# One fused attention and two-mixture kernel on one core: how its first hundred microseconds are fed

## The chip, the cores and the metric

The kernel runs on one core of a Trainium2 chip. The engines of a core run side by side, each through its own queue in order: TensorE (PE, with PEld for its weight loads), VectorE (DVE), ScalarE (ACT), GpSimd (POOL), and SyncE (SP), which here issues the transfers. The metric is the device time of one execution in microseconds, the median of the runs shown.

## The reference

```python
def _attn_ref(q, k, v, s):          # 4 batches, 8 heads, 576 positions, 64 wide, fp32
    scores = scale * np.matmul(q, k.transpose(0, 1, 3, 2))
    cum = np.cumsum(np.maximum(s, 0.0), axis=-1)
    bias = -(cum[:, :, :, None] - cum[:, :, None, :])
    scores = np.where(causal, -1000000000.0, scores + np.minimum(bias, 0.0))
    attn = softmax(scores)
    return np.matmul(attn, v)
def _moe_ref(x, w_in, w_out):       # 2304 tokens, 512 wide, inner width 2048
    h = x @ w_in
    return (h * (1.0 / (1.0 + np.exp(-1.702 * h)))) @ w_out
def _moe2_ref(x, w_in, w_out, s, b):
    r = np.maximum(x @ w_in, 0.0)
    return (s * (r * r) + b) @ w_out
reference = moe2(moe(attention))
```

The weight matrices come in as 64-bit floats and are turned into 32-bit ones on the chip.

## The kernel before, in words

The queries of each batch are cut into a first half (320 positions) and a second (256), which gives eight units; a unit has eight heads, numbered on from unit to unit, so heads 0 to 7 are the first unit. `setup` makes the running sum of the gates, splits it into a rounded part `high` and a rest `low`, and writes these and two constant rows (`root`, `minus`) to a scratch in DRAM, `rows_d`. Each head's operands stand in a tile `raw` (64 rows of queries and keys, `qkT`) with four of these rows beside them, so that one product gives scores and bias together; `prep` loads them (L213, and `beside`, L209 and L210). The first unit's heads are multiplied in plain fp32 (from `raw`); later units use two parts, `hi` and `lo`, in the faster fp32r form.

A head passes through three stages: `qk` (score product L252, row minimum and mask on VectorE L258, exponential on ScalarE L264, scaling by the reciprocal sum), `transposes` (L290, copied out of PSUM at L294 or L296) and `pv` (L311 or L317, copied into `xraw` at L325 or L327). In a step, head n is in `qk`, head n-1 in `transposes`, head n-2 in `pv`. The first unit runs its steps alone. From then on each `run(ui)` works off the mixture of unit `ui` on TensorE and puts the attention stages of the next unit between its matmuls by a table of shares.

The mixture of a unit splits its input `xraw` into two fp32r parts, `xT` (L368 on ScalarE, L369 on VectorE), makes sixteen first-layer sums `ph` (h_item, twelve matmuls each at L385: four blocks of x by three products), and takes tanh (L390), `th` (L391) and a split `g` (L393, L394) of each. After ten of them come four second-layer sums `py` over the first eight g (y_item, L407), then six more `ph`, then the other four `py`. PSUM holds three of these sums at a time.

A weight block is converted by `load_w`: a 512 KB transfer `pair` (L129), L131 on ScalarE, L132 and L133 on VectorE, then a split into two parts, L138 on ScalarE and L139 on VectorE. The sixteen blocks of the first matrix (`wi`) come two to a step from step 1 on. Those of the second (`wo`) are all written after the first unit, ahead of `run(0)`; a staging pool of three `pair` tiles limits them.

Who sets the order: TensorE's queue is as written. SP's is as written in the first unit's steps. Everything else, the `wo` transfers included, is put in place by the framework's scheduler, and a transfer also waits for an earlier one whose completion counter it takes over (eight counters in turn).

Of the kernel before, what the change touches and what calls it, by code (L numbers as in the profile page):

```python
# [9 lines left out]
F32 = mybir.dt.float32  # L10
# [56 lines left out]
def fused_kernel(ctx: ExitStack, tc: tile.TileContext, qkT, vP, s, w1i, w1o, w2i, w2o, s2, b2, out):  # L67
# [75 lines left out]
    with ExitStack() as p1:  # L143
# [15 lines left out]
        def setup():  # L159
            cum = gp.tile([P, 2 * NMAX], F32, tag="g", name="cum")[:BH, :S]  # L160
            nc.sync.dma_start(cum, s)
            zero = gp.tile([P, 2 * NMAX], F32, tag="g", name="zero")[:BH, :S]
# [8 lines left out]
            root = gp.tile([P, 2 * NMAX], F32, tag="g", name="root")[:BH, :S]  # L171
            nc.gpsimd.memset(root, ROOT)
            minus = gp.tile([P, 2 * NMAX], F32, tag="g", name="minus")[:BH, :S]
            nc.gpsimd.memset(minus, -ROOT)
            for side, rows in enumerate(((f32(high), f32(low), minus, minus), (root, root, f32(high), f32(low)))):
                for k, row in enumerate(rows):
                    nc.sync.dma_start(rows_d[side, :, k, :], row)
            nc.sync.dma_start(s_sb, s2.partition_broadcast(P))
            nc.sync.dma_start(b_sb, b2.partition_broadcast(P))
# [18 lines left out]
        def prep(n):  # L198
# [13 lines left out]
            if n < H:  # L212
                nc.sync.dma_start(raw[:D, : u.n + J], src[:D])  # L213
                beside(raw)
            else:
                nc.sync.dma_start(raw[:, : u.n + J], src)
# [145 lines left out]
        def split_x(ui):  # L362
            u = units[ui]
            parts = []
            for cc in range(NC):
                raw = xraw.pop((ui, cc))
                x = xp.tile([P, 2, NMAX], F32R, tag="xT", name="xT")
                nc.scalar.activation(x[:, 0, : u.n], raw[:, : u.n], AF.Copy)  # L368
                nc.vector.tensor_tensor(x[:, 1, : u.n], raw[:, : u.n], f32(x[:, 0, : u.n]), ALU.subtract)  # L369
                parts.append(x)  # L370
            return parts
# [4 lines left out]

        def h_item(ui, f, x):
            n = units[ui].n
            ph = psM.tile([P, 512], F32, tag="m", name="ph1")
            w = wi[f]  # L380
            k = 0
            for cc in range(NC):
                wc = slice(cc * P, (cc + 1) * P)
                for a, b in ((1, 0), (0, 1), (0, 0)):
                    nc.tensor.matmul(ph[:, :n], w[:, a, wc], x[cc][:, b, :n], start=(k == 0), stop=(k == 3 * NC - 1))  # L385
                    k += 1
# [239 lines left out]
```

## Time and profile before

| | us |
|---|---|
| median of 3 runs | 1078.57 (1078.39, 1078.57, 1409.4) |
| profiled execution, its own time | 1075.86 |
| span in the profile, first to last instruction | 1074.1 |

The profiled execution is 2.71 us below the median. The page gives each engine's busy time over the whole span; The views by stretch show where TensorE's share is lower than over the whole; the timeline shows single instructions there.

### The profile page before, as it was taken

To read this page: it belongs to the slowest core of one execution; us is meant where nothing else is said; L and a number is where in the kernel's file an instruction comes from. 1 tells how busy PE (TensorE), PEld (TensorE's weight loads), DVE (VectorE), ACT (ScalarE), POOL (GpSimd) and SP (SyncE) were. 2 spreads that over 40 slices of the span, in tenths; PEclk is the share of its full clock that TensorE was granted. 3 is DMA by queue.
4 is the path that set the end of the run, shared out by engine and by line. 5 is a ranking of instruction groups with operands and counts; after the bars stand their busy time and mean duration, and the time that the engine had idled before them with its cause. 6 is when DMAs were issued, how large, how long until landed. Compare 5 with 4: busy or idle time off the path is not lost.

```text
span 1074.1 us, 17311 instructions
## 1 busy us (share of the span) xinstructions
PE 1020.6 (95%) x6216; PEld 912.4 (85%) x6216; DVE 641.1 (60%) x1440; ACT 536.2 (50%) x1252; POOL 347.2 (32%) x382
## 2 busy tenths in 40 slices
PE   4978999999999999999999998899999999999998
PEld 2457999999989989999999998678888888888887
DVE  4689777566468788878887488942332323232343
ACT  4797766556536646656656476632322322222222
POOL 1224445335335435445444341431301210111011
PEclk9988999999999999999999998999999999999999
DMA  6566322121032232232221187510200100000010
GB/s 200 168 236 200 102 78 77 49 82 55 8 119 73 69 104 70 82 89 71 87 85 50 41 277 236 174 50 1 79 0 1 64 1 1 35 10 1 1 40 20
DMA packets 38917, 85.51 MB, mean 80 GB/s; under 512 B 5520, under 2 KB 16144, under 8 KB 38832
## 3 DMA queue, kind: packets, MB, share of 16 engines
q1 hardware_dynamic: 38832, 84.41, 25.0%
q8 instruction: 49, 0.80, 0.3%
q14 instruction: 36, 0.29, 0.1%
HBM read 70.30 MB, written 10.03 MB: 75 GB/s over the span
## 4 chain that ended last, share of the span: by engine, by line
PE 72%; DVE 12%; ACT 5%; DMA 5%; issue 4%; POOL 1%; SPq 1%; DVEq 0%; ACTq 0%; POOLq 0%
PE py L554 17%; PE ph L506 17%; PE py L407 13%; PE ph L385 12%; PE ps L252 5%; PE pst L290 4%; PE po L317 3%; DVE hi L114 3%; DVE pair L133 1%; DMA pair<-w1i 1%; DVE x L258 1%; ACT x L264 1%; DVE pair L132 1%; DMA pair<-w2i 1%; DMA xraw<-x_d 1%
## 5 line engine op out<-in xcount | busy, mean ns | idle before, releaser
L385 PE MATMUL ph<-xT,wi 128*128 128x320 f32 (+1 forms) x1536 | 245.4, 304 | 7.1 <-ACT xT L368 3.6
L385 PEld LDWEIGHTS ph<-xT,wi 128*128 128x128 f32 x1536 | 216.5, 193 | 8.6 <-ACT xT L368 3.8
L407 PE MATMUL py<-g,wo 128*128 128x320 f32 (+1 forms) x1344 | 215.2, 304 | 1.4 <-DVE th L391 0.9
L554 PE MATMUL py<-wo,g 128*128 128x512 f32 x864 | 209.8, 392 | 5.8 <-POOL g L514 5.8
L506 PE MATMUL ph<-xT,wi 128*128 128x512 f32 (+1 forms) x960 | 208.4, 368 | 0.0
L554 PEld LDWEIGHTS py<-wo,g 128*128 128x128 f32 x864 | 162.2, 189 | 40.4 <-POOL g L514 6.8
L506 PEld LDWEIGHTS ph<-xT,wi 128*128 128x128 f32 x960 | 169.1, 188 | 31.0
L407 PEld LDWEIGHTS py<-g,wo 128*128 128x128 f32 x1344 | 187.9, 189 | 2.6 <-DVE th L391 1.0
L510 DVE TENSOR_TENSOR r<-r 128x512 f32<-128x512 f32 (+1 forms) x80 | 54.2, 678 | 209.4 <-ACT r L509 209.4
L514 POOL TENSOR_TENSOR g<-r,g 128x512 fp32r<-128x512 f32 (+1 forms) x40 | 50.1, 1252 | 314.9 <-PE py L554 170.0
L394 POOL TENSOR_TENSOR g<-th,g 128x320 fp32r<-128x320 f32 (+1 forms) x128 | 112.7, 881 | 113.2 <-ACT g L393 112.7
L264 ACT ACTIVATE x<-x,m 64x64 f32<-64x64 f32 (+2 forms) x160 | 89.5, 560 | 107.7 <-DVE m L258 105.7
L509 ACT ACTIVATE r<-ph 128x512 f32<-128x512 f32 (+1 forms) x80 | 44.3, 553 | 151.3 <-PE ph L506 151.1
L232 POOL TENSOR_TENSOR lo<-raw,hi 64x576 fp32r<-64x576 f32 (+1 forms) x56 | 67.8, 1212 | 136.6 <-issue 59.8
L258 DVE CUSTOM_DVE_ANT_0 x<-ps,mask 64x64 f32<-64x64 f32 (+2 forms) x160 | 68.1, 426 | 60.2 <-PE ps L252 58.3
L290 PE MATMUL pst<-ident,x 128*128 128x128 f32 (+2 forms) x480 | 86.3, 288 | 9.1 <-DVE ph L299 8.4
L513 ACT ACTIVATE g<-r 128x512 fp32r<-128x512 f32 (+1 forms) x80 | 47.0, 587 | 91.9 <-DVE r L511 91.9
L296 ACT ACTIVATE ph<-pst 64x256 fp32r<-64x256 f32 (+2 forms) x144 | 67.0, 472 | 23.3 <-PE pst L290 21.8
L112 POOL TENSOR_SCALAR x<-x,tot 64x64 f32<-64x64 f32 (+1 forms) x96 | 47.9, 506 | 94.1 <-DVE tot L269 70.8
L290 PEld LDWEIGHTS pst<-ident,x 128*128 128x128 f32 (+2 forms) x480 | 54.9, 136 | 24.2 <-DVE ph L299 13.4
L114 DVE TENSOR_SCALAR hi<-raw 128x832 fp32r<-128x832 f32 (+1 forms) x48 | 70.1, 1460 | 2.0 <-DMA vraw<-vP 1.8
L391 DVE SCALAR_TENSOR_TENSOR th<-th,ph 128x320 f32<-128x320 f32 (+1 forms) x128 | 57.4, 448 | 23.0 <-ACT th L390 21.9
(69 smaller groups left out, 1318.0 us busy)
## 6 DMA issues: line engine op xcount, KB each, us to landing
raw<-qkT SPq DMA_DIRECT2D x32, 416.0 KB
pair<-w1o SPq DMA_DIRECT2D x16, 512.0 KB
pair<-w1i SPq DMA_DIRECT2D x16, 512.0 KB
pair<-w2i SPq DMA_DIRECT2D x16, 512.0 KB
pair<-w2o SPq DMA_DIRECT2D x16, 512.0 KB
raw<-qkT SPq DMA_DIRECT2D x24, 320.0 KB
vraw<-vP SPq DMA_DIRECT2D x16, 320.0 KB
out<-y SPq DMA_DIRECT2D x18, 256.0 KB
```

Source lines behind the costliest of these rows:

```text
L114: nc.vector.tensor_scalar(out=out, in0=in_, scalar1=scale, scalar2=None, op0=ALU.mult)
L232: nc.gpsimd.tensor_tensor(lo[:D, kc], raw[:D, kc], f32(hi[:D, kc]), ALU.subtract)
L258: nc.vector.tensor_tensor_reduce(out=x[:w, j0:j1], in0=ps[:w, : j1 - j0], in1=mask[:w, WIDE - a0 + j0 : WIDE - a0 + j1], scale=-1.0 / ROOT ...
L264: nc.scalar.activation(x[:w, :a1], x[:w, :a1], AF.Exp, bias=least, scale=-1.0, accum_out=tot[:w, c : c + 1])
L290: nc.tensor.transpose(ps[: j1 - j0, at : at + a1 - a0], t["x"][c][: a1 - a0, j0:j1], ident[: a1 - a0, : a1 - a0])
L296: nc.scalar.activation(t["ph"][:rows, base:end], ps[:rows, :m], AF.Copy)
L385: nc.tensor.matmul(ph[:, :n], w[:, a, wc], x[cc][:, b, :n], start=(k == 0), stop=(k == 3 * NC - 1))
L391: nc.vector.scalar_tensor_tensor(out=th[:, :n], in0=th[:, :n], scalar=1.0, in1=ph[:, :n], op0=ALU.add, op1=ALU.mult)
L394: nc.gpsimd.tensor_tensor(g[:, 1, :n], th[:, :n], f32(g[:, 0, :n]), ALU.subtract)
L407: nc.tensor.matmul(py[:, :n], wo[f][:, a, wc], g_t[ui, f][:, b, :n], start=(k == 0), stop=(k == 3 * G - 1))
L506: nc.tensor.matmul(ph[:, :n], wi2[f][:, a, wc], x[cc][:, b, :n], start=(k == 0), stop=(k == 3 * NC - 1))
L554: nc.tensor.matmul(py[t], g2[k][a][:, t * P : (t + 1) * P], wo2[k][:, b, :], start=(k == 0 and i == 0), stop=(k == NF - 1 and i == 2),)
```

## The change

1. Head 0's operands no longer pass through DRAM: the constant rows and the first head's `high` and `low` rows are written from SBUF into `raw` by six small transfers, two of them issued by ScalarE. Heads 1 to 7 still read `rows_d`. Head 0's loads, one `wo` block and the constants are queued ahead; the two small loads `s_sb`, `b_sb` move behind step 1.
2. Twenty-seven matmuls (three first-layer sums over the first three blocks of x) are issued between the transposes and the `pv` of head 7. The splits of these three blocks are written there too.
3. `wo` blocks are written one per first-layer sum, in place of all sixteen ahead of `run(0)`.

```diff
--- before.py
+++ after.py
@@ -159,6 +159,18 @@
         def setup():
             cum = gp.tile([P, 2 * NMAX], F32, tag="g", name="cum")[:BH, :S]
             nc.sync.dma_start(cum, s)
+            root = gp.tile([P, 2 * NMAX], F32, tag="g", name="root")[:BH, :S]
+            nc.gpsimd.memset(root, ROOT)
+            minus = gp.tile([P, 2 * NMAX], F32, tag="g", name="minus")[:BH, :S]
+            nc.gpsimd.memset(minus, -ROOT)
+            prep_to(0)
+            u, t = units[0], heads[0]
+            raw = t["parts"][0][0]
+            nc.sync.dma_start(raw[D + 2 : R, t["kc"]], minus[:2, : u.i1])
+            nc.sync.dma_start(raw[D : D + 2, t["qc"]], root[:2, u.i0 : u.i1])
+            for k in range(2):
+                nc.sync.dma_start(rows_d[0, :, 2 + k, :], minus)
+                nc.sync.dma_start(rows_d[1, :, k, :], root)
             zero = gp.tile([P, 2 * NMAX], F32, tag="g", name="zero")[:BH, :S]
             nc.vector.memset(zero, 0.0)
             pos = gp.tile([P, 2 * NMAX], F32, tag="g", name="pos")[:BH, :S]
@@ -168,15 +180,13 @@
             nc.vector.tensor_copy(high, cum)
             low = gp.tile([P, 2 * NMAX], F32R, tag="g", name="low")[:BH, :S]
             nc.vector.tensor_tensor(low, cum, f32(high), ALU.subtract)
-            root = gp.tile([P, 2 * NMAX], F32, tag="g", name="root")[:BH, :S]
-            nc.gpsimd.memset(root, ROOT)
-            minus = gp.tile([P, 2 * NMAX], F32, tag="g", name="minus")[:BH, :S]
-            nc.gpsimd.memset(minus, -ROOT)
-            for side, rows in enumerate(((f32(high), f32(low), minus, minus), (root, root, f32(high), f32(low)))):
-                for k, row in enumerate(rows):
-                    nc.sync.dma_start(rows_d[side, :, k, :], row)
-            nc.sync.dma_start(s_sb, s2.partition_broadcast(P))
-            nc.sync.dma_start(b_sb, b2.partition_broadcast(P))
+
+            for queue, k, part in ((nc.sync, 0, high), (nc.scalar, 1, low)):
+                queue.dma_start(raw[D + k : D + k + 1, t["kc"]], f32(part)[:1, : u.i1])
+                queue.dma_start(raw[D + 2 + k : D + 3 + k, t["qc"]], f32(part)[:1, u.i0 : u.i1])
+            for k, part in enumerate((high, low)):
+                nc.sync.dma_start(rows_d[0, :, k, :], f32(part))
+                nc.sync.dma_start(rows_d[1, :, 2 + k, :], f32(part))
 
         ap, limit = None, 0
         size = {}
@@ -211,7 +221,8 @@
 
             if n < H:
                 nc.sync.dma_start(raw[:D, : u.n + J], src[:D])
-                beside(raw)
+                if n > 0:
+                    beside(raw)
             else:
                 nc.sync.dma_start(raw[:, : u.n + J], src)
             if h % 2 == 0:
@@ -359,33 +370,43 @@
             else:
                 pv(n)
 
-        def split_x(ui):
-            u = units[ui]
-            parts = []
-            for cc in range(NC):
-                raw = xraw.pop((ui, cc))
-                x = xp.tile([P, 2, NMAX], F32R, tag="xT", name="xT")
-                nc.scalar.activation(x[:, 0, : u.n], raw[:, : u.n], AF.Copy)
-                nc.vector.tensor_tensor(x[:, 1, : u.n], raw[:, : u.n], f32(x[:, 0, : u.n]), ALU.subtract)
-                parts.append(x)
-            return parts
+        def split_x(ui, cc):
+            n, raw = units[ui].n, xraw.pop((ui, cc))
+            x = xp.tile([P, 2, NMAX], F32R, tag="xT", name="xT")
+            nc.scalar.activation(x[:, 0, :n], raw[:, :n], AF.Copy)
+            nc.vector.tensor_tensor(x[:, 1, :n], raw[:, :n], f32(x[:, 0, :n]), ALU.subtract)
+            return x
 
         wi, wo = {}, {}
         g_t = {}
         y_t = {}
 
+        begun = {}
+
+        def h_sum(ph, n, f, x, blocks):
+
+            for k in range(3 * blocks.start, 3 * blocks.stop):
+                cc, (a, b) = k // 3, ((1, 0), (0, 1), (0, 0))[k % 3]
+                nc.tensor.matmul(
+                    ph[:, :n], wi[f][:, a, cc * P : (cc + 1) * P], x[cc][:, b, :n],
+                    start=(k == 0), stop=(k == 3 * NC - 1),
+                )
+                if k % 4 == 3 and k < 3 * NC - 1:
+                    yield 4 * (n / 2.4 + 3)
+
+        def h_begin(ui, f, x):
+            ph = begun[ui, f] = psM.tile([P, 512], F32, tag="m", name="ph1")
+            for _ in h_sum(ph, units[ui].n, f, x, range(len(x))):
+                pass
+
         def h_item(ui, f, x):
             n = units[ui].n
-            ph = psM.tile([P, 512], F32, tag="m", name="ph1")
-            w = wi[f]
-            k = 0
-            for cc in range(NC):
-                wc = slice(cc * P, (cc + 1) * P)
-                for a, b in ((1, 0), (0, 1), (0, 0)):
-                    nc.tensor.matmul(ph[:, :n], w[:, a, wc], x[cc][:, b, :n], start=(k == 0), stop=(k == 3 * NC - 1))
-                    k += 1
-                    if k % 4 == 0 and k < 3 * NC:
-                        yield 4 * (n / 2.4 + 3)
+            if (ui, f) in begun:
+                ph = begun.pop((ui, f))
+                yield from h_sum(ph, n, f, x, range(NC - 1, NC))
+            else:
+                ph = psM.tile([P, 512], F32, tag="m", name="ph1")
+                yield from h_sum(ph, n, f, x, range(NC))
             th = gp.tile([P, NMAX], F32, tag="th", name="th", bufs=2)
             nc.scalar.activation(th[:, :n], ph[:, :n], AF.Tanh, scale=0.851)
             nc.vector.scalar_tensor_tensor(out=th[:, :n], in0=th[:, :n], scalar=1.0, in1=ph[:, :n], op0=ALU.add, op1=ALU.mult)
@@ -418,21 +439,25 @@
                 nc.sync.dma_start(x1_d[c * P : (c + 1) * P, t0_of[ui] : t0_of[ui] + n], y[:, :n])
             yield 4 * (n / 2.4 + 3)
 
-        def mixture(ui):
-            x = split_x(ui)
+        def mixture(ui, x):
+            x += [split_x(ui, cc) for cc in range(len(x), NC)]
             for f in range(G + AHEAD):
+                if ui == 0:
+                    load_wo(f)
                 yield from h_item(ui, f, x)
             yield EARLY
             for c in range(NC):
                 yield from y_item(ui, 0, c)
             yield EARLY
             for f in range(G + AHEAD, NF):
+                if ui == 0:
+                    load_wo(f)
                 yield from h_item(ui, f, x)
             yield EARLY
             for c in range(NC):
                 yield from y_item(ui, 1, c)
 
-        def run(ui):
+        def run(ui, x):
 
             lower = H * (ui + 1) if ui in (0, B - 1) else 0
             items = []
...
@@ -454,29 +479,36 @@
 
         with tc.tile_pool(name="half0", bufs=1) as pool, tc.manual_schedule(engines={PE}):
             attention_pool(pool, B * H, 0)
+            x0 = []
             with tc.manual_schedule(engines={PE, SP}):
                 setup()
-                prep_to(0)
                 for step in range(H + 2):
                     for item in attention_items(step):
+                        if item[2] == H - 1 and item[1] == "pv":
+                            x0 += [split_x(0, cc) for cc in range(NC - 1)]
+                            for f in range(3):
+                                h_begin(0, f, x0)
                         if item[2] < H:
                             attend(item)
                     for f in range(len(wi), min(NF, 2 * step)):
                         wi[f] = load_w((wp, "wo", NF), w1i, "wi", f)
-
-            with tc.manual_schedule(engines={PE}):
-                for f in range(NF):
-                    wo[f] = load_w((pool, "pair", 3), w1o, "wo", f)
-                run(0)
+                    if step == 1:
+                        nc.sync.dma_start(s_sb, s2.partition_broadcast(P))
+                        nc.sync.dma_start(b_sb, b2.partition_broadcast(P))
+
+            def load_wo(f):
+                wo[f] = load_w((pool, "pair", 3), w1o, "wo", f)
+
+            run(0, x0)
             for ui in range(1, B - 1):
-                run(ui)
+                run(ui, [])
```

On SP at the program's start (rows of before with before's line numbers, of after with after's) the first stretch reads, before:

```order
L161 DMA cum<-s 32x576
L129 DMA pair<-w1o 128x1024 x3
L177 DMA rows_d<-high 32x576
L177 DMA rows_d<-low 32x576
L177 DMA rows_d<-minus 32x576 x2
L177 DMA rows_d<-root 32x576 x2
L177 DMA rows_d<-high 32x576
L177 DMA rows_d<-low 32x576
L178 DMA s_sb<-s 128x1
L179 DMA b_sb<-b 128x1
L213 DMA raw<-qkT 64x640
L209 DMA raw<-rows_d 4x320
```

and after:

```order
L169 DMA raw<-minus 2x320
L170 DMA raw<-root 2x320
L172 DMA rows_d<-minus 32x576
L173 DMA rows_d<-root 32x576
L172 DMA rows_d<-minus 32x576
L173 DMA rows_d<-root 32x576
L185 DMA raw<-high 1x16x20
L186 DMA raw<-high 1x16x20
L188 DMA rows_d<-high 32x576
L189 DMA rows_d<-high 32x576
L188 DMA rows_d<-low 32x576
L189 DMA rows_d<-low 32x576
```

Ahead of the second piece stand the loads of `cum`, head 0's `raw` and `vraw`, and one `pair`; behind it come head 1's `raw` and its two reads of `rows_d`. Head 0 needs no read of `rows_d` any more.

On TensorE at the end of the first unit (the last `pst` and `po` rows are heads 7's transposes and `pv`) the queue reads, before:

```order
L290 MATMUL pst<-ident,x 128x128 x3
L311 MATMUL po<-ph,vraw 64x320
L311 MATMUL po<-ph,vraw 64x256
L311 MATMUL po<-ph,vraw 64x128
L385 MATMUL ph_780<-xT,wi_216 128x320 x8
L252 MATMUL ps<-lo 64x64
L252 MATMUL ps<-hi 64x64
L385 MATMUL ph_780<-xT,wi_216 128x320 x4
```

and after:

```order
L390 MATMUL ph_645<-xT,wi_218 128x320 x9
L390 MATMUL ph_655<-xT,wi_226 128x320 x9
L390 MATMUL ph_665<-xT,wi_280 128x320 x9
L322 MATMUL po<-ph,vraw 64x320
L322 MATMUL po<-ph,vraw 64x256
L322 MATMUL po<-ph,vraw 64x128
L390 MATMUL ph_645<-xT,wi_218 128x320 x3
L390 MATMUL ph_655<-xT,wi_226 128x320 x3
L263 MATMUL ps<-lo 64x64
L263 MATMUL ps<-hi 64x64
L390 MATMUL ph_665<-xT,wi_280 128x320 x3
```

Twenty-seven matmuls now stand ahead of head 7's `pv`, and nine, in place of thirty-six, are left of these three sums behind it.

On TensorE around the three score products of head 13 (each a `lo` and a `hi` row; 64, 192 and 320 columns) the queue reads, before:

```order
L407 MATMUL py_1323<-g,wo_653 128x320
L252 MATMUL ps<-lo 64x64
L252 MATMUL ps<-hi 64x64
L407 MATMUL py_1323<-g,wo_653 128x320 x2
L407 MATMUL py_1323<-g,wo_661 128x320 x2
L252 MATMUL ps<-lo 128x192
L252 MATMUL ps<-hi 128x192
L407 MATMUL py_1323<-g,wo_661 128x320
L407 MATMUL py_1323<-g,wo_669 128x320 x3
L252 MATMUL ps<-lo 128x320
L252 MATMUL ps<-hi 128x320
```

and after:

```order
L428 MATMUL py_1254<-g,wo_925 128x320 x3
L263 MATMUL ps<-lo 64x64
L263 MATMUL ps<-hi 64x64
L390 MATMUL ph_1334<-xT,wi_522 128x320 x8
L263 MATMUL ps<-lo 128x192
L263 MATMUL ps<-hi 128x192
L390 MATMUL ph_1334<-xT,wi_522 128x320 x4
L263 MATMUL ps<-lo 128x320
L263 MATMUL ps<-hi 128x320
```

Before, the last product of head 13 stands behind 12 of the 24 matmuls of the fourth second-layer sum; after, behind all 24 of it and 12 of the next first-layer sum, so 24 matmuls further on in the mixture.

## Rows read from the trace of the kernel before

**Rows 1.** The page, busy time of each engine over the span:

```profile
PE 1020.6 (95%) x6216; PEld 912.4 (85%) x6216; DVE 641.1 (60%) x1440; ACT 536.2 (50%) x1252; POOL 347.2 (32%) x382
```

**Rows 2.** Stretches: length, busy (PE, PEld, DVE, ACT, POOL), granted clock, DMA share, GB/s:

```profile
0.00:14.57 14.57, 0.00 (x1) 0.01 (x1) 6.87 (x15) 3.36 (x4) 2.50 (x10) 1.00 0.62 189
...
21.09:62.00 40.91, 40.30 (x109) 20.22 (x108) 27.25 (x87) 33.92 (x88) 7.57 (x12) 1.00 0.61 200
...
75.20:107.20 32.00, 26.58 (x147) 24.96 (x147) 29.52 (x72) 25.88 (x66) 12.65 (x16) 0.81 0.54 172
107.20:126.80 19.60, 17.99 (x126) 17.17 (x127) 17.63 (x42) 15.44 (x39) 8.94 (x12) 1.00 0.33 107
126.80:148.00 21.20, 20.77 (x150) 19.80 (x148) 15.71 (x42) 15.16 (x43) 12.81 (x19) 1.00 0.29 79
```

**Rows 3.** The timeline's start, all engines: start us, us, engine, instruction, idle before:

```profile
0.74 0.39 SPq L161 DMA_DIRECT2D cum<-s  x1
...
2.65 0.72 DVE L165 TENSOR_SCALAR pos<-cum 32x576 f32<-32x576 f32 x1 [1.07 <-DMA cum<-s]
...
4.79 0.45 DVE L168 CAST high<-cum 32x576 fp32r<-32x576 f32 x1
5.15 0.68 ACT L131 ACTIVATE pair<-pair 128x512 f32<-128x512 f32 x1 [3.13 <-DMA pair<-w1o]
...
5.50 0.74 DVE L170 TENSOR_TENSOR low<-cum,high 32x576 fp32r<-32x576 f32 x1
...
6.40 0.68 ACT L131 ACTIVATE pair<-pair 128x512 f32<-128x512 f32 x1 [0.57 <-DMA pair<-w1o]
...
8.98 0.43 SPq L177 DMA_DIRECT2D rows_d<-low  x1
...
11.73 0.26 SPq L210 DMA_DIRECT2D raw<-rows_d  x1
...
14.57 2.89 PE L252 MATMUL ps<-raw 68*64 68x64 f32 x8 [14.57 <-DMA raw<-rows_d]
...
21.09 2.48 PE L252 MATMUL ps<-raw 68*64 68x64 f32 x6
...
26.23 1.52 PE L290 MATMUL pst<-ident,x 64*64 64x64 f32 x6
```

**Rows 4.** The timeline, 67 to 76 us, around head 7's `pv`:

```profile
67.47 1.54 PE L311 MATMUL po<-ph,vraw 64*64 64x320 f32 x6 [0.53 <-ACT ph L294]
...
72.62 0.43 ACT L325 ACTIVATE xraw<-po 64x320 f32<-64x320 f32 x1
...
74.25 0.63 PE L385 MATMUL ph<-xT,wi 128*128 128x320 f32 x1 [3.55 <-ACT xT L368]
...
75.17 0.47 DVE L369 TENSOR_TENSOR xT<-xraw,xT 128x320 fp32r<-128x320 f32 x1
```

**Rows 5.** TensorE's groups by form, 10 to 66 us: busy us, mean ns:

```profile
L290 PE MATMUL pst<-ident,x 128*128 128x128 f32 x21 | 5.9, 421 | 0.0
```

**Rows 6.** The same view, 85 to 96 us:

```profile
L290 PE MATMUL pst<-ident,x 128*128 128x128 f32 x3 | 0.5, 273 | 0.0
```

**Rows 7.** The timeline, two full first-layer sums at two granted clocks:

```profile
89.39 2.00 PE L385 MATMUL ph<-xT,wi 128*128 128x320 f32 x12
...
101.03 3.51 PE L385 MATMUL ph<-xT,wi 128*128 128x320 f32 x12
```

**Rows 8.** A stretch in the second sum: length, TensorE busy, granted clock, DMA share, GB/s:

```profile
102.00:103.00 1.00, 1.00 (x5) 0.50 0.78 283
```

**Rows 9.** The timeline, SP's queue at head 10 and TensorE's next head:

```profile
94.65 0.27 SPq L209 DMA_DIRECT2D lo<-rows_d  x1
...
97.08 0.34 SPq L129 DMA_DIRECT2D pair<-w1o  x1
...
97.47 0.33 SPq L210 DMA_DIRECT2D lo<-rows_d  x1
...
105.88 0.20 PE L252 MATMUL ps<-lo 68*64 68x64 f32 x1
```

More of the change, by code (lines that the diff above doesn't have):

```diff
@@ L444, in run @@
             done = 0.0
-            for c in mixture(ui):
+            for c in mixture(ui, x):
                 early, c = (c, 0.0) if c == EARLY else (0.0, c)
@@ L478, in fused_kernel @@
             for ui in range(B - 1, len(units) - 1):
-                run(ui)
+                run(ui, [])
     rawp = ctx.enter_context(tc.tile_pool(name="rawp", bufs=PLACES))
@@ L517, in first_whole @@
     def first_whole(ui):
-        n, x = units[ui].n, split_x(ui)
+        n, x = units[ui].n, [split_x(ui, cc) for cc in range(NC)]
         py = [psY.tile([P, 512], F32, tag="y", name="py3") for _ in range(NC)]
```

## The prediction

> **What bounds the kernel now.** I read the page first: TensorE is busy for 1020.6 of 1074.1 us [rows 1], so an edit that leaves the matmuls alone can win only what TensorE idles. The view by stretch says where the edited part stands: before 14.57 us it has done nothing, and from 75.2 to 107.2 it idles 32.00 - 26.58 = 5.4 us, from 107.2 to 126.8 another 1.6 [rows 2]. Behind that it is nearly full (20.77 of 21.20), and the orders of both kernels soon coincide, so what is won by about 150 us is kept to the end. These stretches and the two long waits between them (0.53 and 3.55 us [rows 4]) hold 14.6 + 0.6 + 5.4 + 1.6 + 0.4 + 4.1 = 26.7 us of idle time, and the first 9 of it can't go (below). A gain of 2% (21.6 us), about what a measurement of this kernel can tell from no change, is thus nearly out of reach.
>
> The timeline then names three limits, one behind the other. At the start it is a chain: gates loaded, VectorE's running sum, eight writes to DRAM, the read back, first product at 14.57 [rows 3]. In the first unit's steps it is TensorE itself (40.30 of 40.91 us) while VectorE has 13.7 us free and ScalarE 7.0 [rows 2]. From 75 us on it is VectorE, busy 29.52 of 32.00 and 17.63 of 19.60 us, mostly with weight conversion; TensorE waits for it there and its clock falls, to 0.81 on average [rows 2].
>
> **Part 1, the start.** `high` is ready at 4.79 + 0.45 = 5.24 us, and `low`, with no conversion between them any more, at 5.24 + 0.74 = 5.98 [rows 3]. SP first issues five loads, of which the `pair` lands late: three of them landed by 5.15 and 6.40 and so on, 1.25 us each [rows 3], and the one that is left now stands behind 352 KB of head 0, 0.87 us at that pace: 6.0. The last of the four constant writes takes over the completion counter of this `pair`, so that SP stands until then; behind it, in SP's order, are both `high` transfers. At 0.43 us an issue [rows 3] the second goes out at 6.9. A small transfer lands 1.9 us after its issue (0.74 to 2.65) or 2.8 (11.73 to 14.57) [rows 3]; halfway, the first product starts at 9.3 instead of 14.57. ScalarE's two issues, at 5.98 and about 6.4, aren't later than that; its table load and first exponential are wanted only after 9.9.
>
> Most of that is lost again at head 1, which still reads `rows_d`. Behind the `high` transfers come two writes of `high`, two of `low`, the load of `raw`, and the read of side 0, which must wait for a write of `low` issued at about 8.7. Such a write was issued at 8.98 and the read behind it left at 11.73, so 2.75 us [rows 3]; then the reads leave at 11.4 and 11.9, the second lands 2.8 us later, and head 1 starts at 14.7. Its product (2.48 us) and head 0's transposes (1.52) [rows 3] then put head 2, which started at 21.09, at 18.5 (its own operands are issued by 13.4 and are in by then). Gain 2.6 us. If the writes land in 1.9 us, head 1 starts at 13.0 and the gain is 4.2; if the `pair` comes 1.5 us later than I think, it is 1.0.
>
> **Between, the steps of the first unit.** They run at TensorE's pace, so the 2.6 us pass through. The two `wo` blocks whose first conversion left the start come here (0.68 us of ScalarE each [rows 3], and by estimate twice that of VectorE); cover is VectorE's 13.7 and ScalarE's 7.0 us of free time [rows 2]. Price 0, and 1 us if it falls just ahead of a copy that TensorE waits for.
>
> **Part 2, 27 matmuls ahead of head 7's `pv`.** Before, TensorE waits 0.53 us for that `pv`, then 3.55 us for the last split of x [rows 4]. The 27 fit into these waits if they run at the higher level: 12 took 2.00 us [rows 7], so 27 take 4.5. The order of ScalarE and VectorE up to that split is nearly that of before; one conversion on each is now ahead of it (0.6 us). The split ends at 75.17 + 0.47 - 2.6 + 0.6, so 2.0 us earlier.
>
> From there VectorE is the limit, so what TensorE has done ahead counts only later. Up to the last score of head 13 (126.8 us before) VectorE has the same list of work in both kernels: the same weight conversions, the same heads, ten `th`. It was busy 47.15 of 51.60 us, so 4.45 us of gaps [rows 2]. With three sums almost done ahead and fewer heads pressed into the first ten sums, half of the gaps should close: 2.2 us (0 to 4.45).
>
> **Part 3, one `wo` block per sum.** It moves conversions from before the second-layer sums to beside them, and changes nothing in the amount. On its own 0; it is why the gaps can close. What it costs is in the slower rival.
>
> **What TensorE has in hand at head 13.** There it stands 24 matmuls further on in the mixture, 24 x 2.00/12 = 4.0 us [rows 7]. Before, the following 21.2 us were TensorE's (20.77) with VectorE at 15.71 [rows 2]; 4.0 us shorter, VectorE would be at 91%, and I take two thirds, 2.7 us (0 to 4.0).
>
> Sum: -2.6 + 0.6 - 2.2 - 2.7 = -6.9 us. The profiled execution of before took 1075.86, so 1069.0; the median lies 2.7 above it, so **1071.7**.
>
> **The clock, read with care.** The granted clock reads 1.00 in the first steps [rows 2], yet the same transposes take 421 ns there [rows 5] and 273 ns between 85 and 96 us [rows 6]. I take the first steps to run at the lower of the two levels, 1.2 GHz, with no record of it, and head 7's `pv` (1.54 us [rows 4]) to be among the first at 2.4. The Trainium skill, "TensorE: Matmul & The Clock Gate", Part 1, says that sustained activity releases the throttle. The rows disagree: TensorE was busy 40.30 of 40.91 us [rows 2] and stayed low. By that rule the 27 matmuls would surely run at the higher level and the next rival would fall away, with the sum as it is.
>
> **Rivals.** First, the 27 matmuls run at the lower level and hold head 7's `pv`. Twelve took 3.51 us there [rows 7], in a stretch at 0.50 [rows 8], so 27 take 7.9. Head 7's transposes end at 67.47 - 0.53 - 2.6 = 64.3; `pv` then starts at 72.2 and takes up to twice 1.54, to 75.3; the copy and split took 3.0 us (72.62 to 75.64) [rows 4], so they end at 78.3, 4.7 us later than I forecast. VectorE stands behind that split in its order. 1071.7 + 4.7 = **1076.4**. For it: the level rose only about when these transposes ran. Against: after head 7's score there is nothing thin between.
>
> Second, everything closes: all 4.45 us of gaps and all 4.0 in hand, -10.5 us, or -12.1 with the better start: **1066.5**. Against it: VectorE's gaps were waits for transfers and TensorE, and some of those stay.
>
> Third, slower: the `wo` transfers, which each wait for a free staging tile, stand in SP's order ahead of the operand copies (`lo`, `hi`, next `raw`) of the heads. Before, one such wait held head 10's second copy from 94.92 to 97.08, 2.2 us [rows 9]; the next head's product came only at 105.88, 8 us after the copies, so it cost nothing. If each of heads 9 to 13 is held so, and the copies have lost that cover, it is 5 x 2.2 = 11 us on -6.9: **1082.5**. It decides once a copy lands after its head's turn on TensorE. Against it: 8 us of cover is much.
>
> **How the numbers follow.** Forecast, 1068 to 1074.5: 0.48. The held `pv`, 1076.4: 0.20. Everything closes, 1066.5: 0.17. Slower, 1082.5: 0.08. The remaining 0.07 lies on both sides outside. The range takes in the first three and the bounds of the start, 1065 to 1078.5, and leaves out about 0.15. Faster by over 2% needs 21.6 where at most some 18 can go, so only a mechanism that I don't see: 0.02. Slower by over 2% needs twice the third rival: 0.01. The rest, 0.97, is within 2%.
>
> **What would show it.** Right: first product near 9.3 us, head 1's near 14.7 (an idle TensorE of about 3 us between), head 2's at 18.5; the last split of x about 2 us earlier than 75.6; VectorE still over 90% busy from there to head 13, whose last score comes 4 us earlier; TensorE idle in that stretch, not behind it. The steps fail in turn if head 1 comes right behind head 0, if `pv` of head 7 starts after 72 us, or if `lo` copies end a wait of TensorE. Most likely to be wrong is the share of VectorE's gaps that closes, and the matmul pace around head 7.

## The result, and the profile after

The median fell from 1078.48 us (the runs of before that were timed beside it) to 1067.81 us in four runs (1066.84 to 1070.49); the ratio is 0.9915, 95% interval 0.9892 to 0.9938, so 9.2 us faster (6.7 to 11.6). One of the four runs of before, 1409.4 us, ran in a slower state and counts in its median but not in the ratio, so the difference of the medians (10.7 us) is not used. Timed again later, with six runs, it was 1067.18 against 1076.63 us: 0.9922 (0.9907 to 0.9937). The forecast was 1071.7, the range 1065 to 1078.5.

The profiled execution of the changed kernel is its slowest of the four (1070.49). Its span is 5.4 us shorter than before's 1074.1: TensorE's busy time has fallen by 2.8 us against [rows 1], its idle time by 2.6.

```profile
span 1068.7 us, 17326 instructions
...
PE 1017.8 (95%) x6216; PEld 910.3 (85%) x6216; DVE 641.3 (60%) x1440; ACT 536.6 (50%) x1252; POOL 347.5 (33%) x382
```

The stretches of that profile, cut at the first product and at the last split of x (columns as in [rows 2]):

```profile
0.00:10.30 10.30, 0.00 (x0) 0.03 (x1) 4.82 (x11) 1.94 (x2) 2.71 (x10) 1.00 0.42 126
10.30:76.12 65.82, 55.92 (x172) 30.73 (x172) 44.69 (x126) 50.11 (x125) 10.52 (x19) 0.77 0.69 225
76.12:108.08 31.96, 27.71 (x171) 26.37 (x171) 31.26 (x73) 28.18 (x71) 15.31 (x19) 0.89 0.55 167
108.08:126.80 18.72, 18.72 (x134) 17.58 (x133) 16.49 (x45) 16.09 (x43) 9.41 (x13) 1.00 0.43 137
...
76.12:185.74 109.62, 104.17 (x708) 99.16 (x708) 91.20 (x234) 81.59 (x217) 54.42 (x73) 0.97 0.38 114
```

The first stretch is 4.3 us shorter than before's 14.57 [rows 3]. Behind the last split VectorE is almost never free (31.26 of 31.96 us), and from 108 us on TensorE is never idle, where before it idled 1.6 us between 107.2 and 126.8 [rows 2]. The last line goes to the first output copy of unit 1, a point at which both kernels have done the same work: before, the same stretch took 115.61 us with 7.6 idle; now it is 109.62 with 5.5 idle. The row of before:

```profile
75.17:190.78 115.61, 108.02 (x723) 103.37 (x724) 93.48 (x235) 81.72 (x217) 53.17 (x73) 0.95 0.35 108
```

Fifteen matmuls that stood behind the split are now ahead of it.

The timeline of the same profile at the start and around the 27 matmuls:

```profile
10.30 2.46 PE L263 MATMUL ps<-raw 68*64 68x64 f32 x6 [10.30 <-DMA raw<-high]
...
14.45 2.45 PE L263 MATMUL ps<-raw 68*64 68x64 f32 x6 [1.69 <-DVE tot L280]
...
18.28 2.48 PE L263 MATMUL ps<-raw 68*64 68x64 f32 x6
...
39.69 1.39 PE L263 MATMUL ps<-raw 68*64 68x64 f32 x4 [2.33 <-DMA raw<-qkT]
...
65.27 1.68 PE L301 MATMUL pst<-ident,x 64*64 64x64 f32 x6 [0.87 <-POOL x L112]
...
66.60 5.51 PE L390 MATMUL ph<-xT,wi 128*128 128x320 f32 x27
...
72.04 1.54 PE L322 MATMUL po<-ph,vraw 64*64 64x320 f32 x6
...
75.74 0.41 PE L390 MATMUL ph<-xT,wi 128*128 128x320 f32 x1 [2.15 <-ACT xT L376]
...
76.12 0.48 DVE L377 TENSOR_TENSOR xT<-xraw,xT 128x320 fp32r<-128x320 f32 x1
```

Head 2 starts 2.8 us earlier than before (18.28 against 21.09 [rows 3]), yet head 7's transposes start where they did (65.27, and before 65.33): TensorE waits in between, longest for head 5's operands (2.33 us at 39.69). Before, that row reads:

```profile
65.33 1.62 PE L290 MATMUL pst<-ident,x 64*64 64x64 f32 x6
```

The 27 matmuls take 5.51 us and push `pv` of head 7 from 67.47 [rows 4] to 72.04, so that the last split of x ends at 76.60, not earlier than before but 1.0 us later.

The second profile, of an execution of 1066.74 us, shows how much of this belongs to one execution:

```profile
7.45 0.59 SPq L186 DMA_DIRECT2D raw<-high  x1
...
9.29 2.45 PE L263 MATMUL ps<-raw 68*64 68x64 f32 x6 [9.29 <-DMA raw<-high]
...
17.01 2.48 PE L263 MATMUL ps<-raw 68*64 68x64 f32 x6
...
63.02 1.68 PE L301 MATMUL pst<-ident,x 64*64 64x64 f32 x6 [2.21 <-POOL x L112]
...
64.35 6.40 PE L390 MATMUL ph<-xT,wi 128*128 128x320 f32 x27
...
70.67 1.54 PE L322 MATMUL po<-ph,vraw 64*64 64x320 f32 x6
...
74.61 0.48 DVE L377 TENSOR_TENSOR xT<-xraw,xT 128x320 fp32r<-128x320 f32 x1
```

Here 2.3 us of the lead are still there at head 7, and the last split ends at 75.10, 0.5 us earlier than before. Program and queues are the same; the start differs by 1 us because the first `pair` is there at 6.40 us in this execution and at 7.40 in the first, and SP, which stands until then, issues the second `high` transfer at 7.45 and at 8.46.

### The profile page after: what moved, and what is told of

Its sections match the earlier page's. It is cut to its first block, busy times and chain, and to the rows that moved or that the text cites. A ratio compares the mean times of both kernels' runs of the same rounds, so it can differ in the third digit from the quotient of the medians.

```text
span 1068.7 us, 17326 instructions
## 1 busy us (share of the span) xinstructions
PE 1017.8 (95%) x6216; PEld 910.3 (85%) x6216; DVE 641.3 (60%) x1440; ACT 536.6 (50%) x1252; POOL 347.5 (33%) x382
## 4 chain that ended last, share of the span: by engine, by line
PE 73%; DVE 12%; DMA 6%; issue 4%; ACT 3%; SPq 1%; POOL 0%; DVEq 0%; ACTq 0%; POOLq 0%
PE py L586 17%; PE ph L538 17%; PE py L428 14%; PE ph L390 13%; PE ps L263 4%; PE pst L301 4%; PE po L328 3%; DMA pair<-w1i 3%; DVE hi L114 3%; DVE pair L133 2%; DVE x L269 1%; ACT x L275 1%; DVE pair L132 1%; DMA pair<-w2i 1%; DMA pair<-w1o 1%
## 5 line engine op out<-in xcount | busy, mean ns | idle before, releaser
L301 PE MATMUL pst<-ident,x 128*128 128x128 f32 (+2 forms) x480 | 85.4, 286 | 11.6 <-DVE ph L310 8.8
L112 POOL TENSOR_SCALAR x<-x,tot 64x64 f32<-64x64 f32 (+1 forms) x96 | 47.3, 500 | 94.9 <-DVE tot L280 69.5
```

The source lines that it names most:

```text
L301: nc.tensor.transpose(ps[: j1 - j0, at : at + a1 - a0], t["x"][c][: a1 - a0, j0:j1], ident[: a1 - a0, : a1 - a0])
```

## The experiments

All are compared with the kernel before on the same chip; times in us against it, worked out from ratio and interval.

**The three parts, on and off.** Seven kernels with every combination of the three parts. Part 1 is taken out by taking back the hunks of the setup, of the load of head 0 and of step 1. Parts 2 and 3 are taken out like this:

```diff
-                        if item[2] == H - 1 and item[1] == "pv":
-                            x0 += [split_x(0, cc) for cc in range(NC - 1)]
-                            for f in range(3):
-                                h_begin(0, f, x0)
                         if item[2] < H:
                             attend(item)
```

```diff
-                if ui == 0:
-                    load_wo(f)
                 yield from h_item(ui, f, x)
...
+            for f in range(NF):
+                load_wo(f)
             run(0, x0)
```

Start alone: 

> The kernel before with the start of the change alone (constants and head 0's rows written from SBUF, one second-matrix block ahead in place of three); the first sums and the second matrix's blocks stay as they were. Theory A, the start's lead is absorbed in the first unit's steps by data that comes no earlier: first product near 10.3 us and head 2's near 18.3, but head 7's transposes again near 65.3, and the time within 1 us of the kernel before (1078). Theory B, the prediction's: the lead passes through, head 7's transposes near 62.5, time 2.6 us lower (about 1075.9).

The 27 matmuls alone: 

> The kernel before with only the 27 matmuls ahead of head 7's pv. Theory A: they run mostly at the lower level, the split of x ends about 1 us later than before's 75.64, yet TensorE has three sums nearly done, the stretch behind gains what VectorE and TensorE idled there, and the time falls by 3 to 6 us (1072.5 to 1075.5). Theory B, the prediction's parts 2 and 'in hand' together: 1074.2 (-4.3). Theory C, the 27 matmuls only move the idle time and the gain of the whole change comes from the second matrix's blocks: 1078, no change.

Second matrix alone: 

> The kernel before with only the second matrix's blocks converted one per first-layer sum. Prediction: 0 on its own (1078.5). Theory A: VectorE's work between 75 and 107 us thins out, scores are computed sooner, and the lower-clock stretch at 97 to 104 us goes: 2 to 5 us lower (1073.5 to 1076.5). Theory D, the slower rival: transfers ahead of operand copies, 2 to 4 us higher.

All but the start: 

> The changed kernel with the start put back as before, parts 2 and 3 kept. Theory A, the start's lead is absorbed: within 1.5 us of the changed kernel (about 1068 to 1069). Theory B, the parts add and the lead passes through: 2.6 us above the changed kernel, 1070.5.

The whole change, again: 

> The changed kernel itself, timed on the chip that the next three run on, with more runs than before. Parts that add (start alone -6.0, parts 2 and 3 together -2.4): -8.4, ratio 0.992. A look at its first steps: the lower-clock stretches lie elsewhere in each run, so its profile may differ from the first by up to 2.5 us, the median not.

All but the 27 matmuls: 

> The changed kernel without the 27 matmuls ahead of head 7's pv (parts 1 and 3). Theory P: the 27 run partly at the lower level and hold pv, with it the last split of x and VectorE's order; taking them out saves 1.5 to 3 us over the whole change (about -10 to -12 against the kernel before). Theory Q: they are worth what the prediction gave TensorE's head start, so leaving them out loses 2 to 3 us (about -6).

All but the spread second matrix: 

> The changed kernel with the second matrix's blocks written all ahead of the mixture as before (parts 1 and 2). By the sum of the single parts: -6.0 - 0.7 = -6.7. Theory P: the same, -6 to -7. Theory Q: the two parts that press TensorE's first sums and the start help each other, -8 to -9.

| start | 27 ahead | wo spread | against before (95%) |
|---|---|---|---|
| x | | | -5.9 (-7.6 to -4.2) |
| | x | | -0.8 (-1.9 to +0.4) |
| | | x | -4.5 (-6.2 to -2.8) |
| | x | x | -2.4 (-3.8 to -1.0) |
| x | | x | -6.9 (-8.9 to -5.0) |
| x | x | | -4.8 (-6.5 to -3.1) |
| x | x | x | -8.4 (-10.0 to -6.8) |

Each part's worth is the mean of four differences (with and without it, the other two held). Start: -5.9, -4.0, -2.4, -6.0, mean **-4.6**. Second matrix: -4.5, -1.6, -1.0, -3.6, mean **-2.7**. The 27 matmuls: -0.8, +2.1, +1.1, -1.5, mean **+0.2**. The mean has an uncertainty of about 1.1 from the spread of the runs alone; what the scheduler's order adds to each kernel (the last experiment) comes on top.

Of the expectations, the start alone fits neither theory: -5.9 is more than theory A's 1 us and more than theory B's 2.6, and so is the 6.0 us that the kernel without the start loses. The 27 matmuls alone fit theory C (no change), the second matrix alone theory A (2 to 5 us). The kernel without the 27, at -6.9, is not faster than the whole, so theory P (they cost 1.5 to 3 us) falls; it lies near theory Q's -6, but its distance of 1.5 us from the whole is within an uncertainty of about 2.5. The kernel without the spread second matrix, at -4.8, is slower than theory Q said; its interval just reaches theory P's -6.

**The 27 matmuls behind `pv` instead of ahead.**

```diff
                         if item[2] == H - 1 and item[1] == "pv":
                             x0 += [split_x(0, cc) for cc in range(NC - 1)]
-                            for f in range(3):
-                                h_begin(0, f, x0)
                         if item[2] < H:
                             attend(item)
+                        if item[2] == H - 1 and item[1] == "pv":
+                            for f in range(3):
+                                h_begin(0, f, x0)
```

> The changed kernel with the same 27 matmuls, but behind head 7's pv in TensorE's queue instead of ahead of it. Theory P: pv starts about 5 us earlier (near 67 us), the last split of x ends some 3 us earlier, the 27 fill the wait for it, and the time is 2 to 3 us below the changed kernel (about -11). Theory Q: no difference, since VectorE is bound by weight conversion there whatever pv does.

Measured -2.4 (-3.8 to -0.9), 6 us slower than the whole change. `pv` did start at 65.46 and the last split at 73.41, both earlier, as theory P wanted; and the time was lost all the same. TensorE's and VectorE's waits from 72 to 125 us (us in total, times, longest):

```profile
PE ph L390 <- DVE th L412: 6.5, 3, 3.5
PE ps L263 <- DVE m L269: 2.1, 1, 2.1
...
DVE pair L132 <- DMA pair<-w1o: 2.2, 4, 0.9
```

In the second profile of the changed kernel the same first row is 1.7 us, and no wait of VectorE for `w1o` is listed. An earlier split is thus not what the stretch lacks. Where the time went can be read up to the sixteenth `th`; the same 384 matmuls of TensorE, first here, then in the second profile of the whole change:

```profile
73.41:142.82 69.41, 60.34 (x384) 57.78 (x383) 55.86 (x140) 52.87 (x134) 32.30 (x40) 0.90 0.40 125
```

```profile
74.61:135.49 60.88, 57.72 (x384) 55.04 (x383) 56.26 (x139) 51.75 (x134) 32.20 (x40) 0.94 0.46 142
```

TensorE idles 9.1 us here and 3.2 there, and its busy time is 2.6 us longer at a lower mean clock (0.90 against 0.94). Its longest wait, 3.5 us, ends with a `th` that stands in VectorE's queue behind conversion steps. VectorE has no more work than in the whole change (55.86 and 56.26 us), but does it in another order.

**How many conversions stand ahead.** In the queue that the scheduler writes for VectorE, 32 conversion steps (L132, L133, L139) stand between the last split and the tenth `th` before, and 26 in the changed kernel; over the eight kernels with the parts on and off the time follows that number (32 for 0, 31 for -0.8 and -2.4, 30 for -4.8, 28 for -5.9 and -4.5, 27 for -6.9, 26 for -8.4). The kernel with `pv` first, with 29 and -2.4, does not fit.

```diff
             for f in range(G + AHEAD):
-                if ui == 0:
+                if ui == 0 and f < G:
                     load_wo(f)
...
-                    load_wo(f)
+                    for _ in range(2 if f < G + 2 * AHEAD else 1):
+                        load_wo(len(wo))
```

> The changed kernel with second-matrix blocks 8 to 15 written only beside the last six first-layer sums (two each beside the first two of them... eight blocks in all, none beside sums 9 and 10). Theory V: what counts is how many weight conversions stand in VectorE's queue ahead of the tenth th; by the queues as built that number is 32 before, 26 in the changed kernel and 29 here, and over the eight kernels with the three parts switched on and off one of them is worth about 1.3 us; so this kernel, although it writes blocks later, is slower than the changed kernel by some 4 us (about -4.5 against before). Theory W: what counts is when the blocks are written in the program; then it is as fast as the changed kernel or faster (-8.4 to -10).

Measured -7.3 (-9.2 to -5.5): 29 conversions ahead and hardly slower than the whole change. Theory V as a rule of one number falls. Theory W (as fast as the changed kernel or faster) is not excluded: the difference of 1.1 us lies within an uncertainty of about 2.4; but nothing was gained.

**One conversion step on GpSimd.**

```diff
-        nc.vector.tensor_tensor(w[:, 1, :], single, f32(w[:, 0, :]), ALU.subtract)
+        engine = nc.gpsimd if src is w1o and f % 2 == 1 and f < G + AHEAD else nc.vector
+        engine.tensor_tensor(w[:, 1, :], single, f32(w[:, 0, :]), ALU.subtract)
```

> The changed kernel with one of the six conversion steps (the last subtraction) of five second-matrix blocks moved from VectorE to GpSimd. VectorE's queue then holds 27 conversions ahead of the tenth th (26 in the changed kernel) and 33 in all up to the sixteenth (37). Theory V by the count ahead: about 1 us slower than the changed kernel (-7). Theory V2, by VectorE's whole load in the stretch: 3 to 4 us of VectorE less, so 2 to 3 us faster (-10.5 to -11.5). Theory X, VectorE and GpSimd slow each other: no gain, VectorE's conversions take longer than 0.68 us.

The step moved is one of a block's five, three of them VectorE's (not one of six). Measured -3.6 (-5.1 to -2.0), 4.8 us slower than the whole change: theory X, and worse than it said. The timeline of this kernel:

```profile
85.95 3.73 DVE L133 SCALAR_TENSOR_TENSOR pair<-pair 128x512 uint32<-128x512 uint32 x1
...
86.19 0.87 POOL L416 TENSOR_TENSOR g<-th,g 128x320 fp32r<-128x320 f32 x1
...
87.02 1.29 POOL L140 TENSOR_TENSOR wo<-pair,wo 128x512 fp32r<-128x512 f32 x1
...
88.28 0.85 POOL L416 TENSOR_TENSOR g<-th,g 128x320 fp32r<-128x320 f32 x1
...
89.88 0.63 PE L264 MATMUL ps<-lo 68*128 68x320 f32 x1 [2.30 <-DVE m L270]
```

VectorE's step takes 0.69 us on average where no GpSimd instruction runs beside it (19 of the 32 in the first 150 us); here it runs for 3.73, until 0.55 us after the third of three GpSimd instructions ends, and TensorE waits behind it. From the last split to the tenth `th` VectorE is busy for 35.09 us with 27 conversions, where the second profile of the changed kernel has 29.75 us with 26. From 75 to 125 us the mean of L133 is 1098 ns here and 933 in the changed kernel's second profile. The Trainium skill, "SBUF — State Buffer", "Summary: rules for kernel authors", says that of a VectorE instruction with two operands in SBUF and a GpSimd instruction that reads SBUF the later one stands until the other is done. These rows agree that one of the two stands, and show more than the page: VectorE's step did not get in between the GpSimd instructions that followed each other.

**The value loads behind the weights.**

```diff
-            if h % 2 == 0:
+            def load_v():
...
+            if h % 2 == 0 and 0 < n < H:
+                late.append(load_v)
+            elif h % 2 == 0:
+                load_v()
...
                         wi[f] = load_w((wp, "wo", NF), w1i, "wi", f)
+                    while late:
+                        late.pop(0)()
```

> The changed kernel with the value loads (vraw) of heads 2, 4 and 6 issued behind the weight loads of their step instead of ahead of them, so that SP does not stand at a value tile while weights could move. Theory A: the first unit's steps wait less for operands (in the changed kernel's first profile 2.3 us for raw, 0.9 for x), the weight conversions come earlier, and VectorE's queue holds 26 ahead of the tenth th but 32 in place of 37 up to the sixteenth: 1 to 3 us faster than the changed kernel (-9.5 to -11.5). Theory V alone: the same as the changed kernel (-8.4).

Measured -6.7 (-8.6 to -4.8): no gain over the whole change. TensorE's long waits for operands are gone from the first steps of its profile, but the 27 matmuls are then done early (from 64.73 us, in 4.30 us), and TensorE waits 4.41 us, up to 74.92 us, for the last split of x.

**An edit that does nothing.**

```diff
-                    if step == 1:
+                    if step == 3:
                         nc.sync.dma_start(s_sb, s2.partition_broadcast(P))
```

> The changed kernel with the two loads of 128 numbers each (s_sb, b_sb, first used after 600 us) issued behind step 3 instead of step 1. By itself this is worth nothing: two issues on SP. But the scheduler's order moves with it: 116 of some 1430 rows of VectorE's queue and 105 of ScalarE's stand elsewhere than in the changed kernel, TensorE's none, and 25 conversions stand ahead of the tenth th in place of 26. Theory V, the count decides: as fast as the changed kernel or 1 us faster (-8.4 to -9.7 against before). Theory O, the order as a whole decides, and any edit draws a new one: it differs from the changed kernel by 2 us or more, most likely upwards (-3 to -6.5), and then differences of 2 us between two of these kernels say nothing about the edit between them.

Measured -5.9 (-7.6 to -4.1): 2.5 us slower than the whole change, with an uncertainty of about 2.4, and timed on another chip. The waits of VectorE and TensorE from 72 to 125 us in its profile, whose execution (1067.24 us) was the fastest of its six and no slower than the whole change, so that they need not show what the others lost:

```profile
PE ph L390 <- ACT xT L376: 5.3, 1, 5.3
...
DVE pair L132 <- DMA pair<-w1o: 2.8, 4, 1.4
...
PE ps L263 <- DMA lo<-hi: 0.7, 1, 0.7
```

So two tiny loads, two steps later, may cost as much as some of the differences above; theory O has one draw for it, with a difference barely outside its uncertainty. The first row shows how the lead is lost here. Head 7's transposes start at 59.58 us, 5.8 us earlier than before, and TensorE is through with `pv` of head 7 at 66.93 us, but the copy of its result on ScalarE, which the split needs, stands behind a conversion of the first matrix that itself waited for VectorE:

```profile
65.39 1.54 PE L322 MATMUL po<-ph,vraw 64*64 64x320 f32 x6
...
70.06 0.67 ACT L138 ACTIVATE wi<-pair 128x512 fp32r<-128x512 f32 x1 [0.86 <-DVE pair L133]
...
70.75 0.43 ACT L336 ACTIVATE xraw<-po 64x320 f32<-64x320 f32 x1
```

No version came out ahead of the changed kernel.

## Why the prediction was right, and where it was not

The direction was right, and the sum of -6.9 came near the measured -8.4 to -9.2. The medians, 1067.8 and 1067.2 us, lie just below the 1068 to 1074.5 that the likeliest case gave itself, nearer to "everything closes" (1066.5). That the sum came so near is in part luck: at the points that the prediction names one term was wrong, one too small and one right. In us against the profile of before:

| stretch | forecast | first profile | second |
|---|---|---|---|
| start to the end of the last split of x | -2.0 | +1.0 | -0.5 |
| from there to the end of head 13's last score | -2.2 | -3.8 | -5.1 |
| from there to the first output copy of unit 1 | -2.7 | -2.2 | -2.2 |
| behind it | 0 | -0.3 | -1.3 |

The rows of the second and third line, of before and then of the second profile of the changed kernel:

```profile
75.17:126.87 51.70, 44.63 (x273) 42.20 (x274) 47.25 (x112) 41.42 (x104) 21.66 (x28) 0.88 0.46 147
126.87:190.78 63.91, 63.38 (x452) 61.16 (x451) 46.23 (x124) 40.30 (x114) 31.51 (x46) 1.00 0.27 77
```

```profile
74.61:121.25 46.64, 43.48 (x282) 41.40 (x282) 45.16 (x112) 40.97 (x106) 23.85 (x28) 0.93 0.52 163
121.25:182.97 61.72, 60.53 (x428) 57.74 (x427) 45.21 (x125) 40.10 (x113) 31.56 (x46) 1.00 0.27 79
```

One execution of each kernel says little, as the two profiles show; pairs of kernels that differ in one part say more. At these points the eight kernels read (us; the last column from the start of the last split to the end of head 13's last score):

| start | 27 ahead | wo spread | head 7's transposes start | last split ends | head 13's last score ends | VectorE idle |
|---|---|---|---|---|---|---|
| | | | 65.33 | 75.64 | 126.87 | 4.45 |
| x | | | 63.76 | 73.92 | 123.60 | 3.23 |
| | x | | 67.02 | 78.89 | 130.13 | 6.29 |
| | | x | 66.51 | 76.83 | 123.44 | 1.66 |
| | x | x | 68.31 | 79.24 | 130.53 | 4.67 |
| x | | x | 63.97 | 73.67 | 120.39 | 2.44 |
| x | x | | 65.37 | 77.26 | 127.88 | 6.66 |
| x | x | x | 63.02 | 75.10 | 121.25 | 1.48 |

**The start, -2.6: passed through, but was worth more.** The first product came at 9.29 and 10.30 us where 9.3 was forecast; the good match of 9.29 is two errors that cancel, for the second `high` transfer left 0.5 us later than forecast (7.45, not 6.9) and took 1.84 us to land, not 2.4. Head 2 started at 18.28 and 17.01 (18.5), so the lead there was 2.8 and 4.1 us. In the four pairs 1.6 to 5.3 us of it are there at head 7, 2.8 on average, and 2.7 at the end of the last split: the lead passes through as forecast. Yet the part is worth 4.6 us as a mean of four. Of the rest, 1.8 us on average are won between the split and head 13's last score. With the start alone VectorE's queue has 28 conversions ahead of the tenth `th` instead of 32, perhaps because the scheduler had other times to plan with; that this is the cause was not shown, and the count failed as a rule (above).

**Part 2, the last split 2.0 us earlier: not so.** The 27 matmuls took 5.51 and 6.40 us, not 4.5, and in all four pairs they put the end of the last split off, by 1.4 to 3.3 us (2.6 on average), where the prediction took them to fit into TensorE's waits. In the first profile `pv` started at 72.04, as the first rival said (72.2), but not for its reasons: the lead was gone there, and the 27 took less than its 7.9 us. That rival also had the price wrong. It took the split to follow `pv` at once, so 4.7 us; but where `pv` starts at 65.4 to 65.9 (with the start alone, without the 27, with `pv` first and in the edit that does nothing) the split still starts only at 72.8 to 73.4, behind weight conversions, so that in the whole change, against the kernel without the 27, a `pv` 5.1 us later puts the split off by only 1.4.

**What TensorE has in hand, -2.7: right.** Behind head 13 TensorE has 24 matmuls less to do (428 and 452 in the rows above), and that stretch is 2.2 us shorter in every profile with the 27, with the start alone or part 3 alone 0.0. The 27 are a wash, +0.2, because what they give there they take at the split, and VectorE's idle time grows with them by 1.8 us on average.

**Part 3, "on its own 0": wrong.** It measured -4.5 alone and -2.7 as a mean. The prediction put the closing of VectorE's gaps, -2.2, down to the 27 matmuls and the later heads, with part 3 only making room for it; it is part 3 that closes them. From the last split to head 13's last score VectorE's idle time falls from 4.45 to 1.66 us with part 3 alone, and by 2.6 us as a mean of the four pairs (0.8 to 5.2). The step "VectorE has the same list of work in both kernels" held at its point: up to head 13's last score there are 38 conversions before and 37 after, and ten `th`. What changed is the order within: ahead of the tenth `th` stand 32 before and 26 after. In the traces that `th` ends at 116.07 before and at 107.43 and 104.68 us after. From the last split to there (before, and then the changed kernel's first profile):

```profile
75.17:116.07 40.90, 35.38 (x209) 33.49 (x210) 38.23 (x87) 33.08 (x82) 18.45 (x23) 0.85 0.54 173
```

```profile
76.12:107.43 31.31, 27.06 (x166) 25.72 (x166) 30.61 (x72) 27.53 (x68) 14.87 (x18) 0.89 0.54 163
```

What left this stretch of VectorE's, 7.6 us of conversions and part of a head's scores, is done from 108 us on, where TensorE is full (18.72 of 18.72) and VectorE has 2.2 us to spare. That this order is how part 3 gains is read from these rows, not shown by an experiment: the number of conversions ahead failed as a rule. TensorE's clock, which fell to 0.50 around 102 us before [rows 8], has no such fall between 85 and 140 us in the two profiles of the whole change.

**The other rivals.** "Everything closes", 1066.5, came close (1067.2 and 1067.8), but neither all gaps (1.9 and 1.5 us are left) nor all of the 4 us in hand (2.2) closed. The slower rival (transfers of the second matrix ahead of operand copies) did not decide: TensorE has no wait for `lo` in the whole change, 0.7 us in the edit that does nothing, and most, 2.3 and 1.6 us, in the two kernels that have the 27 but write the blocks all ahead as before.

**The clock.** That the first steps run at the lower level was an inference from the transposes ([rows 5] against [rows 6]); here it is recorded. From 40 to 65 us of the first profile:

```profile
40.00:65.00 25.00, 23.06 (x60) 10.76 (x58) 18.64 (x50) 21.30 (x53) 6.24 (x10) 0.50 0.54 169
```

TensorE is busy 92% of this stretch and granted 1.2 GHz throughout, and the transposes take 421 ns there too. The Trainium skill, "TensorE: Matmul & The Clock Gate", Part 1, has activity release the throttle; again the row disagrees. The 27 matmuls met both levels in the first profile, 0.50 up to 69.5 us and 1.00 behind it:

```profile
66.60:69.50 2.90, 2.90 (x13) 2.90 (x12) 2.24 (x5) 1.43 (x4) 0.00 (x0) 0.50 0.94 358
69.60:72.11 2.51, 2.51 (x19) 2.32 (x18) 1.91 (x4) 2.14 (x4) 0.00 (x0) 1.00 1.04 408
```

The 4.5 us of the forecast is their price at the higher level, which other executions came near: 4.30 us with the value loads behind the weights and 4.38 in the edit that does nothing.

**What stays open.** Why the start gains 2 us more than its lead, which place in VectorE's order makes `th` late in the kernel with `pv` first, and how much of any single difference of 2 to 3 us here is the edit and how much the order that the scheduler drew with it.

## What to carry to other kernels

Where a scheduler writes the queues, an edit has two effects, its own and a new order on every other engine; measure an edit that should do nothing before believing a difference of its size, and average a part's worth over the other parts switched on and off. Where one engine is full, ask which of its work must be done there at all: what can be moved behind the point where another engine becomes the limit can be a gain without any work saved. Check a forecast term by term, at the points that it names: a sum can be right over terms that are not. Time won ahead of a stretch that waits for transfers is not time won until a row behind that stretch shows it.

## What the runs showed of the hardware

One VectorE instruction, 0.69 us on average where GpSimd stands, ran for 3.73 us while three GpSimd instructions followed each other. Executions of the same program differ by 3.5 us (1066.24 to 1069.72 in six runs); two that were profiled differ by 1 us already at the first product (9.29 and 10.30 us). A granted clock of 1.00 in the profile need not be a record: the transposes of the first steps took 421 ns in a stretch that reads 1.00 [rows 5], where they take 273 at 1.00 later [rows 6], and another execution recorded 0.50 from 40 to 65 us, with 421 ns.
